# One score for each key place modulo 128 in a windowed attention, ahead of fast-matmul expert layers

## The chip, the cores and the metric

The kernel runs on one core of a Trainium2 chip. The metric is the time of one execution on the device, in microseconds (us).

## What is computed

Three layers follow one another. First an attention over 4 batches of 576 tokens with 8 heads of 64 columns; a query sees its own key and the 127 before it, with a linear distance bias by head:

```python
scores = scale * np.matmul(q, k.transpose(0, 1, 3, 2))
rel = pos[:, None] - pos[None, :]
bias = slopes[:, None, None] * (-np.abs(rel).astype(np.float32))[None, :, :]
mask = (rel >= 0) & (rel < 128)
scores = np.where(mask, scores + bias[None], -1000000000.0)
attn = softmax(scores)
return np.matmul(attn, v)
```

Then a mixture of 8 experts on 2304 tokens of width 512 (`relu(x @ w1[e]) @ w2[e]`, weighed by a gate `P` that comes from `exp(x @ w_gate)` by eight rounds of row and column scaling), and last a two-layer network of hidden width 2048 with a leaky ReLU, whose weights come as float64.

## The kernel before

The tokens are cut into 18 tiles of 128. The attention goes tile by tile, and a tile in two quads of four heads, `steps` being the 36 pairs (tile, quad). A tile's keys are its own block of 128 and the block ahead of it, since the window is 128; where a sequence starts at the tile's first token (tiles 0 and 9) there is one block.

For one quad, `scores` (L594) issues four matmuls of 64 rows into two PSUM tiles `s`, each 2 heads x 256 key places. VectorE adds the slope times the distance, with 2**40 in the masked places, and takes the row's minimum in the same operation (L618); ScalarE takes the exponential and the row sum (L622). `probs_T` (L682) transposes `e` on TensorE, 128 columns at a time, into two PSUM tiles `pt`; ScalarE copies one into `pb` (L693), VectorE the other (L695). `values` (L698) multiplies them with the values into `o` (L708), and at the end of a tile VectorE scales `o` by the spread inverse sums `rb` into `acc` (L716). Tiles in which a sequence starts or which stand just behind a start (four of 18) use a `dist` bias of their own (L571 to L580) and scaled queries.

The expert layers use a seven-product scheme (`PRODUCTS`) for 2 x 2 blocks, in float16 high and low parts. Weights are scaled and split by `Weights` (ScalarE L976, L979, L842; GpSimd L843, L1003), inputs by `Inputs` (L842, L843, L894). `a_steps` (L1128) computes the hidden layer, `b_steps` (L1244) the output, which ScalarE (L1251, L1254), VectorE (L1257) and GpSimd (L1255) add into `acc`. Chunk 0 of expert 0 for the first pairs of tiles is woven into the attention by the list `fill`. `logits(p)` (L736) multiplies a pair's split inputs with the gate weights; for pairs 3 and 4 it is called right after the attention (L1401).

What order all this runs in is set by the class `Plan`: it reads the program's instructions, gives each a cost (`weigh`), finds what depends on what (`depend`), gives each a latest time from the order of TensorE's work (`deadlines`), lists each engine's instructions greedily (`order`), and fixes that list by dependencies. So a change to a cost, or to the program, may move instructions on all engines.

Of the kernel before, what the change touches and what calls it, by code (L numbers as in the profile page):

```python
# [26 lines left out]
FIRST = (0, 1, 3)  # L27
# [3 lines left out]
class Plan:  # L31
# [13 lines left out]
    LANDING = 2000.0  # L45
    PER_NS = 350.0
# [78 lines left out]
    def weigh(self, node, kind, reads, writes):  # L125
# [6 lines left out]
        if "DMA" in kind:  # L132
            sizes = [x[1][0][1] * x[4] * x[3] for x in reads + writes if x[0].split("_")[0] != "in"]
            node["cost"], node["landing"] = max(sizes) / self.PER_NS, self.LANDING
# [30 lines left out]
        elif eng == "Pool":  # L165
            node["cost"] += 190 + 1.89 * n if "float16" in kinds else 185 + 2.12 * n
# [8 lines left out]
    def depend(self, slots, before, after):  # L175
# [11 lines left out]
        for i, node in enumerate(self.nodes):  # L187
# [9 lines left out]
            for name, (r, w) in touched.items():  # L197
# [26 lines left out]
                for mask, k, wrote in seen.get(name, []):  # L224
                    if mask & ((r | w) if wrote else w):
                        found.add(k)
                    if mask & ~w:
                        kept.append((mask & ~w, k, wrote))
# [49 lines left out]
    def order(self, latest):  # L278
# [3 lines left out]
        ready, free = [0.0] * n, dict.fromkeys(self.START, 0.0)  # L282
        waiting = {eng: [] for eng in self.START}
# [23 lines left out]
        def takes(i, t):  # L307
# [3 lines left out]
            if node["eng"] == "PE":  # L311
                cost += self.TURN.get((mode, node["mode"]), 0)
            elif node["shared"] and gpsimd[0] <= t < gpsimd[1]:
                cost = max(cost, gpsimd[1] - t + cost - node["shared"])
            return cost

        for _ in range(n):
# [39 lines left out]
            end = start + cost  # L357
            if eng == "PE":
# [11 lines left out]
            free[eng] = end - (self.START[eng] if cost > 100 else 0)  # L370
            waiting[eng].remove(pick)
# [46 lines left out]
def attn_moe_kernel(  # L418
# [24 lines left out]
    BIG = float(2**40)  # L443
# [43 lines left out]
    qscale = new(const, [P, NP], F32, name="qscale")  # L487
# [13 lines left out]

    for h in range(H):
        r = 64 * (h % 2)
        nc.gpsimd.memset(qscale[r:r + 64, h // 2:h // 2 + 1], -(D ** -0.5) * 2.0 ** (8.0 * (h + 1) / H))


# [25 lines left out]
    def small_psum(shape, name):  # L532
        if "ps_bx" in pools:
# [12 lines left out]
    ramp = new(ap1, [P, 2, 2 * P], F32, tag="e", bufs=4, name="e")  # L546
    dist = ramp[:, 0]
    nc.gpsimd.iota(dist, pattern=[[-1, 2 * P]], base=P, channel_multiplier=1, allow_small_or_imprecise_dtypes=True)
    nc.gpsimd.affine_select(out=dist, in_=dist, pattern=[[1, 2 * P]], base=0, channel_multiplier=-1,
                            compare_op=ALU.is_gt, fill=BIG)  # L550
    nc.gpsimd.affine_select(out=dist, in_=dist, pattern=[[-1, 2 * P]], base=P, channel_multiplier=1,
                            compare_op=ALU.is_ge, fill=BIG)
    slopes = new(ap1, [P, H, 2 * P], F32, name="slopes")
    for h in range(H):
        nc.scalar.activation(out=slopes[:, h], in_=dist, func=AF.Copy, scale=-8.0 * 2.0 ** (-8.0 * (h + 1) / H))

# [5 lines left out]
    def load_qk(i):  # L562
# [5 lines left out]
        st["keys"] = nc.sync.dma_start(k_t[:, :, 0:w], kv[:, :, t0 + P - w:t0 + P])  # L568
        kb = [i] if t0 % S == 0 else [i - 1, i]
        crossed = t0 // S != (t0 + P - 1) // S  # L570
        bias = None  # L571
        if crossed or t0 % S == S - 4 * P:

            bias = new(ap1, [P, 2 * P], F32, tag="dist", name="dist")
            nc.scalar.activation(out=bias, in_=slopes[:, 0], func=AF.Copy, scale=-0.125 * 2.0 ** (8.0 / H))
            if crossed:
                nc.gpsimd.memset(bias[64:128, 0:192], BIG)
            else:
                nc.gpsimd.memset(bias[:, 0:64], BIG)
            nc.gpsimd.tensor_tensor(out=q_t, in0=q_t, in1=qscale.unsqueeze(2).to_broadcast([P, NP, P]), op=ALU.mult)  # L580
        st[i] = dict(k=k_t, qs=q_t, kb=kb, bias=bias)
# [11 lines left out]

    def scores(i, quad):  # L594
        c = st[i]
        kb, qs = c["kb"], c["qs"]
        W = P * len(kb)
        c0 = 2 * P - W
# [5 lines left out]
        e = [new(ap1, [P, 2, 2 * P], F32, tag="e", bufs=4, name="e") for _ in range(2)]  # L604
        c[quad] = dict(e=e)
        for n in range(2):
            for r in range(2):
                h = 4 * quad + 2 * n + r
                ins = nc.tensor.matmul(s[r][:, n, 0:W], qs[64 * r:64 * r + 64, h // 2, :],
                                       c["k"][64 * r:64 * r + 64, h // 2, 0:W], start=True, stop=True)  # L610
        exps = c[quad]["exps"] = []
        for r in range(2):
            for n in range(2):
                h = 4 * quad + 2 * n + r
                bias, scale = slopes[:, h], -0.125
                if c["bias"] is not None:
                    bias, scale = c["bias"], 2.0 ** (-8.0 * (h + 1) / H)
                nc.vector.tensor_tensor_reduce(  # L618
                    out=e[r][:, n, 0:W], in0=s[r][:, n, 0:W], in1=bias[:, c0:], scale=scale,
                    scalar=float(2**41), op0=ALU.add, op1=ALU.min, accum_out=mn[:, 2 * n + r:2 * n + r + 1],  # L620
                )
                ins = nc.scalar.activation(  # L622
                    out=e[r][:, n, 0:W], in_=e[r][:, n, 0:W], func=AF.Exp, bias=mn[:, 2 * n + r:2 * n + r + 1],
                    scale=-1.0, accum_out=sm[:, h:h + 1],
                )
            exps.append(ins)
# [55 lines left out]
    def probs_T(i, quad):  # L682
        c = st[i][quad]
        nb = len(st[i]["kb"])
        c["pb"] = []
        for r in range(2):
            pt = new(ps_t, [P, 2, 2, P], F32, tag="pt", name="pt")
            for n in range(2):
                for b in range(nb):
                    ins = nc.tensor.transpose(pt[:, n, b, :], c["e"][r][:, n, b * P:(b + 1) * P], ident)  # L690
# [842 lines left out]
```

## Time and profile before

| what | value |
|---|---|
| median of three runs | 1840.01 us |
| the three runs | 1840.07, 1840.01, 1834.02 us |
| the profiled execution | 1834.78 us |
| its span, first to last instruction | 1833.0 us |
| TensorE busy | 1807.0 us (99%) |
| ScalarE busy | 1350.1 us (74%) |
| VectorE busy | 1329.2 us (73%) |
| GpSimd busy | 1310.8 us (72%) |
| granted TensorE clock, mean | 0.997 |

PE is TensorE's matmuls, PEld its weight loads, DVE VectorE, ACT ScalarE, POOL GpSimd, SP the engine that issues the loads. The durations of matmuls overlap, so what a matmul costs is read from when the next one starts. The attention lies in the first 177 us of the span.

### The profile page before, as it was taken

Reading aid. Unit: us, or ns where it says so; the run is one execution under the profiler, and the core shown is the slowest. Engines: PE = TensorE matmul, PEld = TensorE weight load, DVE = VectorE, ACT = ScalarE, POOL = GpSimd, SP = SyncE. Lnnn points to the kernel's source line nnn. Section 1 sums busy time; section 2 is a strip of 40 time slices with the busy share of each in tenths; the row PEclk is TensorE's granted clock in tenths of the full one; section 3 lists DMA queues with packets and bytes.
Section 4 is the critical chain, followed back from the end, with each engine's and each line's share of the span. In section 5 each row is a group of like instructions: output and inputs, shape, how many; then the busy total and the mean of one; then the engine's idle time right before and its main releaser. Section 6 shows DMA issues by size and latency. Waiting matters only on the chain.

```text
span 1833.0 us, 45057 instructions
## 1 busy us (share of the span) xinstructions
PE 1807.0 (99%) x17542; PEld 1603.2 (87%) x17542; DVE 1329.2 (73%) x3656; ACT 1350.1 (74%) x3099; POOL 1310.8 (72%) x1154
## 2 busy tenths in 40 slices
PE   8999999999999999999999999999999999999999
PEld 6677888889989898988989898989899888989888
DVE  6877677767777676777777667666666887777877
ACT  8989778767767767767767766667666789877664
POOL 3854778787869777787868777666766796776653
PEclk9999999999999999999999999999999999999999
DMA  8342020202112021202111120100001000101002
GB/s 292 106 130 75 2 82 30 87 19 82 53 47 67 34 73 39 87 19 81 53 47 54 46 82 6 43 24 24 24 24 48 1 25 24 47 2 47 2 33 73
DMA packets 61094, 97.80 MB, mean 53 GB/s; under 512 B 4560, under 2 KB 27600, under 8 KB 60880
## 3 DMA queue, kind: packets, MB, share of 16 engines
q1 hardware_dynamic: 60880, 94.93, 15.7%
q8 instruction: 137, 2.24, 0.5%
q14 instruction: 77, 0.63, 0.1%
HBM read 81.81 MB, written 13.11 MB: 52 GB/s over the span
## 4 chain that ended last, share of the span: by engine, by line
PE 71%; ACT 2%; DVE 2%; DMA 1%; POOL 1%; issue 0%; SPq 0%; ACTq 0%
PE t L1244 36%; PE s L1128 20%; PE sq L1128 15%; DMA raw<-in_moe_w_dram 1%; DVE sx L930 0%; DVE s L1156 0%; ACT acc L917 0%; POOL w L843 0%; ACT junk L976 0%; ACT h L1197 0%; PE xt L916 0%; POOL h L1200 0%; DVE acc L1257 0%; ACT raw L979 0%; ACT q L1140 0%
## 5 line engine op out<-in xcount | busy, mean ns | idle before, releaser
L1244 PE MATMUL t<-w,h 128*128 128x256 f16 x7560 | 949.3, 273 | 5.1 <-ACT acc L1251 3.2
L1128 PEld LDWEIGHTS <-w 128*128 128x128 f16 x8400 | 756.4, 98 | 89.3 <-issue 9.4
L1244 PEld LDWEIGHTS <-h 128*128 128x128 f16 x7560 | 735.1, 98 | 92.6 <-issue 7.5
L1128 PE MATMUL s<-xp,w 128*128 128x256 f16 (+1 forms) x4872 | 591.3, 262 | 2.6 <-ACT q L1140 1.3
L1257 DVE SCALAR_TENSOR_TENSOR acc<-t,pu,acc 128x256 f32<-128x256 f32 x866 | 406.6, 479 | 179.0 <-PE t L1244 151.0
L1200 POOL TENSOR_TENSOR h<-s,h 128x1024 f16<-128x1024 f32 x180 | 383.9, 2133 | 132.1 <-ACT h L1197 76.2
L1128 PE MATMUL sq<-xp,w 128*128 128x256 f16 (+1 forms) x3528 | 429.4, 262 | 1.9 <-DVE s L1156 1.1
L1255 POOL TENSOR_TENSOR acc<-acc,part 128x256 f32<-128x256 f32 x322 | 234.3, 729 | 194.3 <-ACT part L1254 75.7
L843 POOL TENSOR_TENSOR w<-raw,w 128x512 f16<-128x512 f32 x240 | 274.9, 1162 | 46.6 <-ACT w L842 46.4
L1140 ACT ACTIVATE q<-s 128x256 f32<-128x256 f32 x364 | 138.9, 382 | 135.9 <-PE s L1128 133.2
L1197 ACT ACTIVATE h<-s 128x1024 f16<-128x1024 f32 x180 | 190.1, 1056 | 47.0 <-DVE s L1156 45.5
L1156 DVE SCALAR_TENSOR_TENSOR h<-sq,h 128x512 f16<-128x512 f32 x352 | 193.0, 553 | 30.5 <-ACT h L1175 24.4
L1254 ACT ACTIVATE part<-t,pu 128x256 f32<-128x256 f32 x322 | 151.7, 471 | 76.3 <-PE t L1244 71.6
L1144 DVE SCALAR_TENSOR_TENSOR sq<-s,q 128x256 f32<-128x256 f32 x176 | 75.9, 431 | 149.1 <-PE s L1128 91.9
L1144 DVE SCALAR_TENSOR_TENSOR sq<-sq,q 128x256 f32<-128x256 f32 x352 | 150.2, 427 | 37.7 <-PE sq L1128 34.3
L842 ACT ACTIVATE w<-raw 128x512 f16<-128x512 f32 x240 | 148.1, 631 | 12.3 <-PE s L1128 3.9
L1156 DVE SCALAR_TENSOR_TENSOR s<-sq,s 128x256 f32<-128x256 f32 x352 | 146.1, 415 | 0.7
L1175 ACT ACTIVATE h<-sq 128x512 f16<-128x512 f32 x176 | 104.7, 595 | 56.2 <-DVE sq L1144 47.1
L1156 DVE SCALAR_TENSOR_TENSOR s<-sq,q 128x256 f32<-128x256 f32 x352 | 136.7, 417 | 10.6 <-ACT q L1152 8.8
L976 ACT ACTIVATE junk<-raw 128x512 bf16<-128x512 f32 x160 | 100.8, 630 | 11.9 <-DMA raw<-in_moe_w_dram 8.4
L979 ACT ACTIVATE raw<-raw,sr 128x512 f32<-128x512 f32 x160 | 108.4, 719 | 0.1
L1003 POOL TENSOR_TENSOR raw<-raw 128x512 f32<-128x512 f32 x80 | 102.0, 1275 | 0.4 <-DVE dg L819 0.4
(151 smaller groups left out, 1643.1 us busy)
## 6 DMA issues: line engine op xcount, KB each, us to landing
raw<-in_moe_w_dram SPq DMA_DIRECT2D x32, 768.0 KB, 4.7
k_t<-in_k_dram SPq DMA_DIRECT2D x16, 512.0 KB, 4.1
raw<-in_moe_w_dram SPq DMA_DIRECT2D x32, 256.0 KB, 3.6
raw<-in_moe_w_in_dram SPq DMA_DIRECT2D x16, 512.0 KB, 3.6
raw<-in_moe_w_out_dram SPq DMA_DIRECT2D x16, 512.0 KB, 3.5
q_t<-in_q_dram SPq DMA_DIRECT2D x18, 256.0 KB, 3.0
acc<-in_v_dram SPq DMA_DIRECT2D x18, 256.0 KB, 6.0
v_t<-in_v_dram SPq DMA_DIRECT2D x18, 256.0 KB, 2.9
```

The costliest lines, as they stand in the source:

```text
L842: nc.scalar.activation(out=hi, in_=src, func=AF.Copy)
L843: return nc.gpsimd.tensor_tensor(out=lo, in0=src, in1=hi, op=ALU.subtract)
L1128: nc.tensor.matmul(d[b][:, f, :], t[:, wp, kk, ft * P:(ft + 1) * P], XP[p][:, o, kk, xp, :], start=(i == 0 and f == 0 and j in FIRST), sto ...
L1140: nc.scalar.activation(out=q[:, k], in_=ps, func=AF.Copy, scale=CS)
L1144: nc.vector.scalar_tensor_tensor(out=block(k), in0=ps, scalar=CS, in1=q[:, k], op0=ALU.mult, op1=ALU.add)
L1156: nc.vector.scalar_tensor_tensor(out=out, in0=in0, scalar=sc, in1=in1, op0=op0, op1=op)
L1197: nc.scalar.activation(out=h[:, 3:7, 0, :], in_=d["s"], func=AF.Copy)
L1200: nc.gpsimd.tensor_tensor(out=h[:, 3:7, 1, :], in0=d["s"], in1=h[:, 3:7, 0, :], op=ALU.subtract)
L1244: nc.tensor.matmul(ps, h[:, o, hp, f, tt * P:(tt + 1) * P], w[:, wp, ft, :], start=(i == 0 and j in FIRST), stop=(i == 5), skip_group_chec ...
L1254: nc.scalar.activation(out=part, in_=ps, func=AF.Copy, scale=s)
L1255: nc.gpsimd.tensor_tensor(out=dst, in0=dst, in1=part, op=ALU.add)
L1257: nc.vector.scalar_tensor_tensor(out=dst, in0=ps, scalar=s, in1=dst, op0=ALU.mult, op1=ALU.add)
```

## The change

In the attention, a key place of the own block and the same place of the block ahead are never both inside a query's window: own-block keys count up to the query's place, block-ahead keys behind it. The change keeps one score for the two. `scores` still computes 256 places. Then a predicated copy on VectorE writes the scores of the block ahead over those of the own block where the mask `ahead` is 1, in PSUM, for two heads at once. Tiles in which a sequence starts, or behind which one started, get an operation that drops the places outside the sequence. Distance, minimum, exponential, sum and transposes then run on 128 places a head in place of 256. After the transposes, which now fill one PSUM tile for four heads, the probabilities are parted again: ScalarE copies all of them, GpSimd clears the own block's places by an affine selection, and the result goes with the values of the block ahead; VectorE multiplies them by the mask `own` for the values of the own block. The `dist` biases and the scaled queries go.

Besides, the planner gets other constants (DMA landing time and rate, a start time of SP's queue, slower matmuls in its first 11.5 us, a cost of its own for GpSimd's fixed operations) and one rule: two instructions of different engines on one PSUM tile are ordered, reads too. The logits of pairs 3 and 4 move from behind the attention into the list of gating jobs, eight and nine ticks later than they stood; the gate itself starts two ticks earlier.

```diff
-    LANDING = 2000.0
-    PER_NS = 350.0
+    LANDING = 2250.0
+    FIRST = 740.0
+    PAUSE = 1200.0
+    COLD = 11500.0
...
+                    elif mask and name in self.whole and self.nodes[k]["eng"] != node["eng"]:
+                        found.add(k)
...
-    slopes = new(ap1, [P, H, 2 * P], F32, name="slopes")
+    slopes = new(ap1, [P, H, P], F32, name="slopes")
...
-            nc.gpsimd.tensor_tensor(out=q_t, in0=q_t, in1=qscale.unsqueeze(2).to_broadcast([P, NP, P]), op=ALU.mult)
...
+    def drop(x, mask):
+        nc.vector.scalar_tensor_tensor(out=x, in0=spread(mask, x.shape[2]), scalar=-BIG, in1=x, op0=ALU.mult, op1=ALU.add)
...
-        e = [new(ap1, [P, 2, 2 * P], F32, tag="e", bufs=4, name="e") for _ in range(2)]
+        e = [new(ap1, [P, 2, P], F32, tag="e", bufs=6, name="e") for _ in range(2)]
...
         for r in range(2):
+            mine = s[r][:, :, P:2 * P]
+            if at:
+                nc.vector.copy_predicated(mine, spread(ahead, P).bitcast(I32), s[r][:, :, 0:P])
+            if at == 0:
+                drop(mine, ahead)
+            elif S - P < at:
+                drop(mine[64:128], other[64:128])
+            elif at < P:
+                drop(mine[0:64, :, 0:64], ahead[0:64, 0:64])
             for n in range(2):
                 h = 4 * quad + 2 * n + r
...
                 nc.vector.tensor_tensor_reduce(
-                    out=e[r][:, n, 0:W], in0=s[r][:, n, 0:W], in1=bias[:, c0:], scale=scale,
+                    out=e[r][:, n], in0=mine[:, n], in1=slopes[:, h], scale=-0.125,
...
     def probs_T(i, quad):
         c = st[i][quad]
-        nb = len(st[i]["kb"])
-        c["pb"] = []
+        pt = new(ps_t, [P, 4, P], F32, tag="pt", name="pt")
         for r in range(2):
-            pt = new(ps_t, [P, 2, 2, P], F32, tag="pt", name="pt")
             for n in range(2):
-                for b in range(nb):
-                    ins = nc.tensor.transpose(pt[:, n, b, :], c["e"][r][:, n, b * P:(b + 1) * P], ident)
-            pb = new(ap3, [P, 2, 2, P], F32, tag="pb", name="pb")
-            if r == 0:
-                nc.scalar.activation(out=pb[:, :, 0:nb, :], in_=pt[:, :, 0:nb, :], func=AF.Copy)
+                nc.tensor.transpose(pt[:, 2 * r + n, :], c["e"][r][:, n], ident)
+        part = [None, None]
+        for b in range(2 - len(st[i]["kb"]), 2):
+            pb = part[b] = new(ap3, [P, 4, P], F32, tag=f"pb{b}", bufs=2, name="pb")
+            if b == 0:
+                nc.scalar.activation(out=pb, in_=pt, func=AF.Copy)
+                nc.gpsimd.affine_select(out=pb, in_=pb, pattern=[[0, 4], [-1, P]], base=0, channel_multiplier=1,
+                                        compare_op=ALU.is_gt, fill=0.0)
             else:
-                nc.vector.tensor_copy(pb[:, :, 0:nb, :], pt[:, :, 0:nb, :])
-            c["pb"].append(pb)
+                nc.vector.tensor_tensor(out=pb, in0=pt, in1=own.unsqueeze(1).to_broadcast([P, 4, P]), op=ALU.mult)
+        c["pb"] = part[2 - len(st[i]["kb"]):]
...
-    for p in (3, 4):
-        logits(p)
-        tick()
-    gating += [None] * 16 + gate()
+    gating += [None] * 8 + [lambda: logits(3), None, lambda: logits(4)] + [None] * 5 + gate()
```

Counts over the whole program: transposes 272 to 144; reductions of 256 columns 128 to 0, of 128 columns 16 to 144; copies of `pb` on VectorE 36 to 0, products into `pb` 0 to 36; predicated copies 0 to 64; dropping operations 0 to 24; selections of `pb` on GpSimd 0 to 32; query products on GpSimd 4 to 0. The matmuls of the scores, the values, the experts and the network, and the transfers, are the same in number.

The order shows the change at three places. TensorE, early in the attention, before (`s` are scores, `pt` transposes, `o` values, `rt` the spreading of the inverse sums):

```order
L690 MATMUL pt<-ident,e 128x128 x4
L708 MATMUL o<-pb,v_t 64x128 x8
L674 MATMUL rt<-ident,sm 64x128 x8
L609 MATMUL s<-k_t,q_t 128x256 x4
L690 MATMUL pt<-ident,e 128x128 x8
L708 MATMUL o<-pb,v_t 64x128 x8
L690 MATMUL pt<-ident,e 128x128 x4
L609 MATMUL s<-k_t,q_t 128x256 x4
```

and now:

```order
L695 MATMUL pt<-ident,e 128x128 x4
L613 MATMUL s<-k_t,q_t 128x256 x4
L682 MATMUL rt<-ident,sm 64x128 x8
L695 MATMUL pt<-ident,e 128x128 x4
L613 MATMUL s<-k_t,q_t 128x256 x4
L717 MATMUL o<-pb,v_t 64x128 x16
L695 MATMUL pt<-ident,e 128x128 x4
L613 MATMUL s<-k_t,q_t 128x256 x4
```

A quad had eight transposes in two pieces and has four in one; the values follow later, two quads at a time.

VectorE, the scores of one quad, before (an `ISA` row with `e,mn` is the reduction, the one behind it reads its minimum):

```order
L618 ISA e,mn<-s,slopes 128x256
L618 ISA mn 128x1
L618 ISA e,mn<-s,slopes 128x256
L618 ISA mn 128x1
L825 TENSOR_REDUCE k<-mt 128x1
L695 COPY pb<-pt 128x512
```

and now:

```order
L618 COPY_PREDICATED s<-ahead,s 128x2x128 x2
L627 ISA e,mn<-s,slopes 128x128
L627 ISA mn 128x1
L627 ISA e,mn<-s,slopes 128x128
L627 ISA mn 128x1
L627 ISA e,mn<-s,slopes 128x128
L627 ISA mn 128x1
L627 ISA e,mn<-s,slopes 128x128
L627 ISA mn 128x1
L834 TENSOR_REDUCE k<-mt 128x1
L704 TENSOR_TENSOR pb<-pt,own 128x512
```

Two predicated copies stand ahead of four shorter reductions, and the copy of `pb` is a product.

ScalarE, behind the attention's end, before (`xp` are the splits of the last inputs, `acc<-t,pu` evacuates the expert output):

```order
L842 ACTIVATE xp_2803<-acc_111 128x4x128
L842 ACTIVATE xp_2803<-acc_113 128x2x128
L842 ACTIVATE xp_2803<-sx 128x8x128
L842 ACTIVATE xp_2804<-acc_114 128x4x128
L842 ACTIVATE xp_2804<-acc_115 128x2x128
L842 ACTIVATE xp_2804<-h 128x8x128
L1251 ACTIVATE acc_102<-t_2945,pu 128x256
```

and now:

```order
L851 ACTIVATE xp_2729<-acc_110 128x4x128
L851 ACTIVATE xp_2729<-acc_112 128x2x128
L851 ACTIVATE xp_2729<-sx 128x8x128
L851 ACTIVATE xp_2730<-acc_113 128x4x128
L1260 ACTIVATE acc_101<-t_2801,pu 128x256
L851 ACTIVATE xp_2730<-acc_114 128x2x128
L1184 ACTIVATE h<-sq 128x2x256
L1161 ACTIVATE q<-s_2791 128x256
L851 ACTIVATE xp_2730<-h 128x8x128
L1260 ACTIVATE acc_101<-t_2801,pu 128x256
```

The first evacuation stood behind nine splits (three are ahead of these rows) and stands behind seven.

## Rows read from the trace of the kernel before

**Rows 1.** Busy time by stretch: from:to, length, busy us (instructions), clock, DMA, GB/s.
```profile
core 0: us, PE busy (x) PEld busy (x) DVE busy (x) ACT busy (x) POOL busy (x), PEclk, DMA share, GB/s
0.00:37.00 37.00, 29.91 (x255) 22.06 (x255) 24.89 (x114) 29.29 (x103) 7.35 (x24) 0.95 0.94 317
37.00:75.00 38.00, 33.49 (x308) 24.72 (x308) 29.51 (x113) 36.35 (x105) 32.59 (x34) 0.96 0.42 135
75.00:107.00 32.00, 31.60 (x357) 25.62 (x353) 24.56 (x86) 29.02 (x87) 24.91 (x30) 1.00 0.42 135
107.00:137.00 30.00, 29.59 (x284) 22.88 (x281) 22.57 (x82) 27.24 (x89) 10.31 (x15) 1.00 0.32 98
137.00:159.00 22.00, 21.58 (x286) 17.23 (x288) 17.22 (x68) 20.97 (x67) 13.30 (x18) 1.00 0.44 137
159.00:177.00 18.00, 18.00 (x200) 14.34 (x197) 15.16 (x57) 15.58 (x52) 1.00 (x4) 1.00 0.10 27
...
300.00:600.00 300.00, 299.55 (x2906) 269.71 (x2904) 215.92 (x552) 217.31 (x471) 236.31 (x202) 1.00 0.18 57
```

**Rows 2.** Waits of TensorE, 0 to 177 us: total us, times, longest.
```profile
PE s L609 <- DMA k_t<-in_k_dram: 4.6, 1, 4.6
PE pt L690 <- ACT rb L680: 2.5, 2, 1.8
PE pt L690 <- ACT pb L693: 2.1, 2, 1.1
```

**Rows 3.** Timeline, TensorE: start us, length us, line, operation, count.
```profile
170.47 1.09 PE L690 MATMUL pt<-ident,e 128*128 128x128 f32 x8
...
173.17 0.66 PE L690 MATMUL pt<-ident,e 128*128 128x128 f32 x4
```

**Rows 4.** Timeline, VectorE, first quads: reductions one after another.
```profile
5.92 0.29 DVE L618 CUSTOM_DVE_ANT_0 e<-s,slopes 128x128 f32<-128x128 f32 x1 [4.78 <-PE s L609]
6.14 0.29 DVE L618 CUSTOM_DVE_ANT_0 e<-s,slopes 128x128 f32<-128x128 f32 x1
...
11.67 0.42 DVE L618 CUSTOM_DVE_ANT_0 e<-s,slopes 128x256 f32<-128x256 f32 x1
...
12.02 0.42 DVE L618 CUSTOM_DVE_ANT_0 e<-s,slopes 128x256 f32<-128x256 f32 x1
```

**Rows 5.** Timeline, ScalarE, first quads: exponentials one after another.
```profile
6.65 0.39 ACT L622 ACTIVATE e<-e,mn 128x128 f32<-128x128 f32 x1
...
7.04 0.39 ACT L622 ACTIVATE e<-e,mn 128x128 f32<-128x128 f32 x1
...
12.61 0.50 ACT L622 ACTIVATE e<-e,mn 128x256 f32<-128x256 f32 x1
...
13.10 0.49 ACT L622 ACTIVATE e<-e,mn 128x256 f32<-128x256 f32 x1
```

**Rows 6.** Groups by form, whole span: count | busy us, mean ns | idle before.
```profile
L1144 DVE SCALAR_TENSOR_TENSOR sq<-s,q 128x256 f32<-128x256 f32 x176 | 75.9, 431 | 149.1 <-PE s L1128 91.9 <-ACT q L1140 52.7 <-ACT raw L1075 1.3
...
L1172 DVE TENSOR_TENSOR sq<-sq,q 128x512 f32<-128x512 f32 x36 | 25.1, 698 | 5.7 <-ACT q L1171 4.3
...
L695 DVE COPY pb<-pt 128x512 f32<-128x512 f32 x32 | 21.9, 685 | 3.1 <-ACT e L622 1.1 <-PE o L708 1.1 <-PE pt L690 0.3
...
L693 ACT ACTIVATE pb<-pt 128x512 f32<-128x512 f32 x32 | 18.9, 589 | 1.9 <-PE pt L690 1.4
...
L580 POOL TENSOR_TENSOR q_t<-q_t,qscale 128x512 f32<-128x512 f32 x4 | 4.2, 1041 | 30.4 <-DMA k_t<-in_k_dram 17.9 <-PE o L708 7.2 <-PE rt L678 3.4
...
L637 POOL TENSOR_SCALAR_AFFINE_SELECT sel<-sel 128x512 bf16<-128x512 bf16 x3 | 2.0, 667 | 0.2
...
L549 POOL TENSOR_SCALAR_AFFINE_SELECT e<-e 128x256 f32<-128x256 f32 x1 | 0.4, 401 | 0.1
```

**Rows 7.** Timeline behind the attention: TensorE and ScalarE, with idle time before.
```profile
176.37 1.48 PE L1244 MATMUL t<-w,h 128*128 128x256 f16 x12
...
181.78 1.04 ACT L842 ACTIVATE xp<-h 128x1024 f16<-128x1024 f32 x1
...
183.23 2.71 PE L1244 MATMUL t<-w,h 128*128 128x256 f16 x12 [2.94 <-ACT acc L1251]
```

## The prediction before the run

> **What bounds the kernel now.** I read the busy time by stretch first, then the waits, the single instructions, and at last the place behind the attention. From 300 to 600 us TensorE is busy for 299.55 of 300 us [rows 1]: the expert layers run at TensorE's pace, and a change to the attention cannot shorten them. The attention fills the first 177 us. I cut that time where three more of the 18 query tiles have their output; each of the first six rows is such a stage, with three tiles or six quads (a quad is four heads of one tile). In the first two stages TensorE is idle for 37.00 - 29.91 = 7.1 us and 38.00 - 33.49 = 4.5 us; in the other four for 1.2 us in all. The tightest engine beside it is ScalarE: 36.35 of 38.00 us in the second stage, 20.97 of 22.00 in the fifth. Added up over the six stages: ScalarE 158.5 us, VectorE 133.9, GpSimd 89.5, of 177. So VectorE has the most room among the two engines that can read PSUM, and the change moves work onto it. TensorE's longest waits on an engine in this stretch name ScalarE (2.5 us for the spread inverses, 2.1 us for a probability copy, both ahead of transposes) [rows 2].
>
> **TensorE.** 272 transposes become 144: 128 fewer. Eight in a row took 1.09 us and four 0.66 us [rows 3], so one costs (1.09 - 0.66) / 4 = 0.109 us, and 128 cost 14.0 us, 2.3 us a stage. Nothing else on TensorE gets shorter: scores still run over 256 columns and values over both blocks. The Trainium skill, "TensorE: Matmul & The Clock Gate", Part 4, gives about 275 ns for a PE-mode transpose in one kernel; counted that way the saving would be 128 x 0.275 = 35 us (an estimate from that page). By the start times above it is 14.0 us: the page's figure is a latency, and neighbours overlap.
>
> **ScalarE.** 128 of 144 exponentials fall from 256 to 128 columns. They start 0.49 us apart at 256 columns and 0.39 at 128 [rows 5]: 128 x 0.10 = 12.8 us less. The copies of probabilities stay 32 of 512 columns; four 256-wide ones and four bias copies go, some 3 us more at the most. ScalarE: 158.5 - 13 to 16, about 143 us.
>
> **VectorE.** 128 reductions fall from 256 to 128 columns: starts 0.35 us apart against 0.21 [rows 4], so 128 x 0.14 = 17.9 us less. 36 copies become 36 products of 512 columns out of PSUM: 0.698 against 0.685 us [rows 6], 0.5 us more, and 1 us more for the four that were narrow. New are 64 predicated copies of 2 x 128 columns inside PSUM. The trace has none. The nearest row has the same shape, PSUM in and PSUM out: 0.431 us [rows 6], and I take that: 27.6 us. Bounds: below, 0.21 us, the step of the reduction over half the columns, 13.4 us; above, 0.698 us, the product over twice the columns [rows 6], 44.7 us. The Trainium skill, "VectorE: DVE Perf Modes", in its section on the errata, has 120 + FD cycles for a PSUM source, (120 + 256) / 0.96 = 392 ns here, by which the 64 would cost 25.1 us (estimate from that page). 24 masking operations of at most 256 columns, at the same 0.431: 10.3 us. Four one-off masks: 1.7 us at most. Net: -17.9 + 1.5 + 27.6 + 10.3 + 1.7 = +23.2 us, 3.9 us a stage; VectorE goes from 133.9 to 157 us and takes ScalarE's place as the tightest engine beside TensorE.
>
> **GpSimd.** 32 new selections over 512 f32 columns. Such a selection took 0.401 us over 256 columns and 0.667 over 512 of bf16 [rows 6]; so 0.667 to 0.802 for twice 0.401; I take 0.667, the row with as many columns: 21.3 us, 3.6 us a stage (25.7 at the upper end). Four query products of 1.041 us [rows 6] go, two each in stages two and five. That fits into 89.5 of 177 us, but stage two is already at 32.59 of 38.00.
>
> **Chain of a quad.** Before, the two halves of the transposed probabilities lay in two PSUM tiles: ScalarE copied one (0.589 us) while VectorE copied the other (0.685) [rows 6]. Now both read one tile, and the selection follows ScalarE's copy: 0.589 + 0.667 on one side, or 0.589 + 0.698 where the two reads take turns, so about 0.6 us more from transposes to values. Where the expert layers have matmuls to put between, this is covered; that is not so at the very start and in the last stage, whose 18 us hold few of them.
>
> **By stage.** A stage can't be shorter than its fullest engine, which I let run at 95%, the share that ScalarE reached in stages two and five. First: VectorE 24.89 + 3.9 and the 6 us before its first reduction [rows 4] make 35; TensorE 37 - 2.3 = 34.7: -2.0. Second: GpSimd 32.59 + 3.6 - 2.1 = 34.1, VectorE 33.4; over 0.95, 36: -2.0. Third: VectorE 28.5, GpSimd 28.5, so TensorE decides: -2.3. Fourth: VectorE 26.5, TensorE 27.7, -2.3. Fifth: VectorE 17.22 + 3.9 = 21.1, over 0.95 = 22.2: +0.2. Sixth: 15.16 + 3.9 = 19.1, over 0.95 = 20.1: +2.1. Sum -6.3: of TensorE's 14.0 us, 7.7 are not cashed.
>
> **Behind the attention.** TensorE is idle for 2.94 us before 183.23, waiting for ScalarE's first evacuation of the expert output, which stands behind nine splits (the last 1.04 us long); then 12 matmuls take 2.71 us where 12 took 1.48 at 176.37 [rows 7]. With the logits of pairs 3 and 4 later, the order puts that evacuation ahead of the last two splits. It gains at least the last split, 1.0 us, at most 2.94 + 1.23 = 4.2; I take 2.7, between. The 60 small logits matmuls and their three small followers each are the same in number; they fall in a stretch where TensorE has a backlog, and cost nothing unless the gating behind them comes late. The DMAs are the same transfers; the third tile's query and key now go ahead of the first value tile on SP's queue, which I cost at nothing: TensorE waits for a load once, for 4.6 us at the very start [rows 2].
>
> **Sum.** -6.3 - 2.7 = -9.0. The profiled execution took 1834.78 us (span 1833.0), so 1825.8; the three runs have 1834.02, 1840.01 and 1840.07, with the median 5.2 above the profiled one. On the median: 1840.0 - 9.0 = **1831 us**.
>
> **Rivals.**
> *VectorE keeps up.* The planner may spread the expert layers' matmuls so that no stage is VectorE's. Then all 14.0 us count, the waits of [rows 2] go (4.6) and so does the whole end stall (4.2): -22.8, 1817 us. For it: VectorE needs 157 us of some 163. Against it: 96% over the whole stretch, where ScalarE got 89%. Chance 0.19.
> *The chain eats it.* ScalarE's copy and VectorE's product of the one tile take turns, and the selection stands in GpSimd's queue among products of over 1 us: 0.6 us more a quad, exposed in a third of the 36 quads, gives back 7.2 us of the 9.0: 1838 us. For it: no second tile is there any more to read meanwhile. Against: TensorE was idle for 1.2 us only in the last four stages, so it has other matmuls to put there. Chance 0.24. The Trainium skill, "PSUM — Partial Sum Buffer", in the section on PSUM bank collisions, says that two engines must not access the same partitions of one bank at the same time, whether or not they touch the same bytes; by that the turns are forced. No row of before shows two engines at one tile of probabilities.
> *Slower: predicated copies near their upper bound.* At 0.698 us VectorE needs another 64 x 0.267 = 17.1 us, 174 in all; at 95% with the 6 us of the start that is 189 us where the attention had 177: +12 - 2.7, 1849 us. It turns where the attention's gain is gone: VectorE at 163 us, 0.53 us a copy. For it: no row of before holds that operation. Against: the PSUM rows follow their columns (0.431 at 256, 0.698 at 512). Chance 0.12.
> That the change does less than it says can be excluded for the counts, which the order shows.
>
> **Numbers.** Forecast 0.45 (1820 to 1836), keeping up 0.19, chain 0.24, slower 0.12. Changes under about 0.5% (9.2 us) can't be told from none here. Faster by more, under 1830.8: 0.19 and 0.6 of 0.45, together 0.46 (its lower side is longer, since the range of the end stall and of the copies reach further down). Same: the other 0.18, and the chain's 0.24, less 0.02: 0.40. Slower: 0.14. The range 1814 to 1843 leaves out the slower case and a little at the lower end.
>
> **What would show it.** Right: transposes 144 and the attention's last output at 170 to 173 us; VectorE over 88% busy in the last two stages, ScalarE under 85%; TensorE's waits there naming VectorE; the 2.94 us wait gone or halved. Wrong: VectorE under 80% with TensorE waiting on GpSimd's selection (the chain), a predicated copy over 0.53 us (slower), or the attention ending before 165 us with TensorE at 97% (keeping up). The end of the program, from 300 us on, should be as before within 2 us; if it is not, the new order outside the attention is the cause, which I have not priced.

## The result, and the profile after

The changed kernel takes 1815.87 us (median of four runs, 1815.47 to 1816.65) where the kernel before took 1837.31 beside it (four runs, 1834.02 to 1840.07). The ratio is 0.9885, 95% interval 0.9867 to 0.9904; a second comparison (whole_again, below) gave 0.9894 (0.9881 to 0.9907). It is faster by 1.1%, 21 us by the medians, where 9 were forecast. By the profiled executions it is 18.7 us: 1834.78 to 1816.09, spans 1833.0 and 1814.4.

Busy time by stretch, after, cut again where three more tiles have their output, with a stretch of the expert layers at the end (compare [rows 1]):

```profile
core 0: us, PE busy (x) PEld busy (x) DVE busy (x) ACT busy (x) POOL busy (x), PEclk, DMA share, GB/s
0.00:33.20 33.20, 26.26 (x225) 20.11 (x227) 24.11 (x121) 23.30 (x94) 7.67 (x18) 1.00 0.90 292
33.20:74.10 40.90, 37.61 (x314) 27.02 (x310) 35.03 (x159) 36.54 (x121) 32.12 (x36) 0.83 0.58 188
74.10:107.70 33.60, 32.40 (x340) 26.31 (x337) 29.81 (x114) 30.48 (x100) 29.44 (x35) 0.95 0.45 143
107.70:132.80 25.10, 24.24 (x242) 19.03 (x240) 21.29 (x86) 21.48 (x72) 12.14 (x17) 1.00 0.30 97
132.80:155.50 22.70, 22.33 (x282) 17.25 (x283) 21.25 (x97) 21.34 (x84) 19.00 (x26) 1.00 0.36 109
155.50:169.00 13.50, 13.45 (x164) 11.02 (x163) 11.66 (x39) 7.37 (x25) 3.32 (x8) 1.00 0.10 35
286.00:586.00 300.00, 299.37 (x2904) 269.39 (x2902) 215.44 (x548) 217.64 (x471) 237.10 (x202) 1.00 0.18 57
```

The attention ends at 169.0 us, with the last scaling of `o` into `acc`, where it ended at 177.3. Summed over it, VectorE is busy for 143.2 us, ScalarE for 140.5, GpSimd for 103.7; before, 134.2, 158.5 and 89.5. So VectorE took 9 us more, not the 23.2 of the forecast. The stretch of the expert layers is as full as before. TensorE's idle time up to the attention's end is the same, 12.8 us before ([rows 1]) and 12.7 after; its busy time fell from 164.2 to 156.3 us, by 8 us where 14.0 us of transposes went. The granted clock was 0.83 in the second stage and 0.95 in the third, where no stage before was under 0.95; the last section comes back to that.

TensorE's waits from 0 to 169 us, after (total us, times, longest):

```profile
PE s L613 <- DVE mn L627: 5.8, 6, 1.6
PE s L613 <- DMA k_t<-in_k_dram: 5.0, 1, 5.0
PE mt L832 <- DVE dg L828: 0.7, 1, 0.7
PE pt L695 <- ACT e L631: 0.7, 1, 0.7
```

The two waits that named ScalarE [rows 2] are gone. In their place TensorE waits for VectorE's reductions, which hold the PSUM tile that the next scores need: 5.8 us. No wait names GpSimd's selection.

Groups of the new and the shortened operations, after, whole span (count | busy us, mean ns | idle before):

```profile
L627 DVE CUSTOM_DVE_ANT_0 e<-s,slopes 128x128 f32<-128x128 f32 x144 | 34.0, 285 | 0.9 <-PE pt L695 0.6
L618 DVE COPY_PREDICATED s<-ahead,s 128x256 f32<-128x256 int32 x64 | 24.8, 425 | 10.7 <-PE s L613 10.3
L704 DVE TENSOR_TENSOR pb<-pt,own 128x512 f32<-128x512 f32 x36 | 24.3, 683 | 1.3 <-ACT pb L700 1.0 <-ACT rb L688 0.2
L597 DVE SCALAR_TENSOR_TENSOR s<-other,s 64x256 f32<-64x256 f32 x8 | 3.2, 438 | 0.1
L701 POOL TENSOR_SCALAR_AFFINE_SELECT pb<-pb 128x512 f32<-128x512 f32 x32 | 20.6, 648 | 38.4 <-ACT pb L700 37.6 <-DVE s L1165 0.5
L631 ACT ACTIVATE e<-e,mn 128x128 f32<-128x128 f32 x144 | 56.0, 392 | 11.6 <-DVE mn L627 9.4 <-PE rt L682 2.0
```

A predicated copy takes 0.425 us, next to the 0.431 that was taken for it; a selection 0.648, next to 0.667; a product 0.683, next to 0.698 [rows 6]. The prices were right for one instruction alone. Neighbours overlap, though, as the timeline of VectorE, after, shows (start us, length us):

```profile
34.34 0.42 DVE L618 COPY_PREDICATED s<-ahead,s 128x256 f32<-128x256 int32 x1
34.67 0.15 DVE L843 TENSOR_SCALAR sr<-k 128x1 int32<-128x1 int32 x1
34.73 0.42 DVE L618 COPY_PREDICATED s<-ahead,s 128x256 f32<-128x256 int32 x1
```

The instruction behind the copy starts 0.33 us after it, not 0.42. If each moment is counted once, for the instruction that was there first, the 64 copies take 23.8 us of VectorE's time (0.371 each).

Behind the attention, after: TensorE, then ScalarE, with the idle time before (compare [rows 7]):

```profile
171.37 0.82 PE L1137 MATMUL sq<-xp,w 128*128 128x256 f16 x6
173.65 0.82 PE L1253 MATMUL t<-w,h 128*128 128x256 f16 x6 [1.46 <-ACT acc L1260]
175.79 0.81 PE L1253 MATMUL t<-w,h 128*128 128x256 f16 x6 [1.33 <-DVE acc L1266]
...
172.62 0.61 ACT L851 ACTIVATE xp<-acc 128x512 f16<-128x512 f32 x1
173.14 0.45 ACT L1260 ACTIVATE acc<-t,pu 128x256 f32<-128x256 f32 x1
```

The wait of 2.94 us has become 1.46, and a second one of 1.33 for VectorE stands behind it.

A difference that no step of the forecast holds lies near the end of the program, where the last network begins. Waits of TensorE from 1430 to 1560 us, before:

```profile
PE xt L916 <- DVE k L828: 1.6, 1, 1.6
PE t L1244 <- DVE acc L1257: 1.3, 2, 0.9
PE sq L1128 <- DVE s L1156: 0.7, 2, 0.4
```

Busy time there, before, and then after (its stretch with nearly the same matmuls begins 14 us earlier):

```profile
1430.00:1560.00 130.00, 125.83 (x1182) 112.05 (x1181) 107.24 (x309) 111.97 (x245) 103.46 (x81) 1.00 0.05 18
```

```profile
1416.00:1540.00 124.00, 123.98 (x1180) 111.85 (x1177) 106.30 (x309) 109.98 (x245) 103.21 (x81) 1.00 0.05 19
```

1180 matmuls take 124 us where 1182 took 130, and the 4.2 us in which TensorE was idle there are gone. So some 5 of the 18.7 us of the profiled executions, over a quarter, lie 1250 us behind the attention.

### The profile page after: what moved, and what is told of

Same layout as the page of the kernel before. It is cut to its first block, busy times and chain, and to the rows that moved or that the text cites. A ratio compares the mean times of both kernels' runs of the same rounds, so it can differ in the third digit from the quotient of the medians.

```text
span 1814.4 us, 45033 instructions
## 1 busy us (share of the span) xinstructions
PE 1794.3 (99%) x17414; PEld 1595.6 (88%) x17414; DVE 1341.7 (74%) x3748; ACT 1330.1 (73%) x3091; POOL 1325.5 (73%) x1170
## 4 chain that ended last, share of the span: by engine, by line
PE 91%; DMA 3%; DVE 2%; ACT 2%; POOL 1%; issue 1%; SPq 0%; POOLq 0%; ACTq 0%; DVEq 0%
PE t L1253 42%; PE s L1137 25%; PE sq L1137 18%; PE s L613 2%; PE o L717 2%; DMA raw<-in_moe_w_dram 1%; DMA raw<-in_moe_w_in_dram 1%; PE pt L695 1%; PE xt L925 0%; PE rt L682 0%; POOL raw L1090 0%; ACT junk L985 0%; DVE s L1165 0%; POOL w L852 0%; POOL raw L1086 0%
```

## Experiments: the parts alone

The change was taken apart: the attention, the planner's rule for two engines on one PSUM tile, the planner's constants and costs, and the place of the logits. The planner makes a new order for each kernel. The kernels were compared in three groups, each beside the kernel before, so rows are compared by their ratios; by the intervals, two rows have to differ by some 3 to 5 us to be told apart. The last column is (1 - ratio) x 1836 us, about the median of before in the three groups.

| kernel | attention | rule | constants | logits | ratio to before (95%) | us gained |
|---|---|---|---|---|---|---|
| rule_only | old | new | old | old | 0.9976 (0.9965 to 0.9988) | 4.4 |
| consts_only | old | old | new | old | 0.9972 (0.9961 to 0.9984) | 5.1 |
| plan_only | old | new | new | old | 0.9940 (0.9922 to 0.9958) | 11.0 |
| logits_only | old | old | old | new | 0.9968 (0.9956 to 0.9979) | 5.9 |
| plan_logits | old | new | new | new | 0.9952 (0.9938 to 0.9966) | 8.8 |
| attn_rule | new | new | old | old | 0.9969 (0.9955 to 0.9983) | 5.7 |
| no_logits | new | new | new | old | 0.9922 (0.9903 to 0.9940) | 14.3 |
| whole_again | new | new | new | new | 0.9894 (0.9881 to 0.9907) | 19.5 |

**attn_rule**, the attention with the rule:

```diff
-    LANDING = 2250.0
-    FIRST = 740.0
-    PAUSE = 1200.0
-    COLD = 11500.0
+    LANDING = 2000.0
+    FIRST = 0.0
+    PAUSE = 0.0
+    COLD = 0.0
...
-    gating += [None] * 8 + [lambda: logits(3), None, lambda: logits(4)] + [None] * 5 + gate()
+    for p in (3, 4):
+        logits(p)
+        tick()
+    gating += [None] * 16 + gate()
```

The costs of transfers and of GpSimd's fixed operations are back as well.

> The new attention with the planner's old constants and the logits back behind the attention; of the planner's edits only the rule for two engines on one PSUM tile stays. Theory 1 (the attention pays by itself, 12 us ahead of 300 us, of which 3 to 4 hang on the logits; the 6 us of TensorE's idle time near 1440 to 1550 us are the planner's): 8 to 10 us faster than before, ratio 0.9945 to 0.9955, and the idle time near 1440 to 1550 us still 5 to 7 us. Theory 2 (the gain is the planner's new order, the transposes were hidden): within 4 us of before, ratio 0.998 to 1.002. Theory 3 (the late idle time goes with the attention, by whatever reordering it brings): 15 to 18 us faster, ratio 0.990 to 0.992.

It gained 5.7 us, between theories 1 and 2, and TensorE was busy for all of 1430 to 1560 us, so the idle time there is gone without the constants. Since rule_only gains 4.4 without the new attention, the attention adds 1.3 here, less than the intervals can tell from nothing. Theory 1 falls in this form.

**plan_only**, the old attention with the planner of the change:

```diff
+                    elif mask and name in self.whole and self.nodes[k]["eng"] != node["eng"]:
+                        found.add(k)
...
+        free["SP"] = self.FIRST
...
-                cost += self.TURN.get((mode, node["mode"]), 0)
+                cost += self.TURN.get((mode, node["mode"]), 0) + (0.9 * cost if t < self.COLD else 0)
```

These are three places of its edit, which is the whole class `Plan` of the change, with all constants and costs.

> The old attention and the old place of the logits, with all of the planner's edits. Theory 1: the 6 us of idle time near 1440 to 1550 us go and little else changes: 5 to 7 us faster than before, ratio 0.996 to 0.9973. Theory 2 (the gain is the planner's): 14 us faster or more, ratio under 0.9925. Theory 3 (the planner's edits do nothing): within 2 us, ratio 0.999 to 1.001.

11.0 us: more than theory 1 had, short of theory 2, and by itself half of the whole gain, from a part that the forecast put at nothing.

**rule_only** and **consts_only**, which split it:

```diff
+                    elif mask and name in self.whole and self.nodes[k]["eng"] != node["eng"]:
+                        found.add(k)
```

(and, for consts_only, the new class without these two lines)

> The kernel before with one edit: the planner's rule that orders two engines on one PSUM tile, reads too. Theory 1 (the rule's order removes TensorE's 6 us of idle time near 1440 to 1550 us, the constants act in the first 200 us): 5 to 7 us faster, ratio 0.996 to 0.9975, that idle time under 1 us, the first 200 us as before. Theory 2 (the constants do both): within 2 us of before, ratio 0.999 to 1.001, that idle time still 5 to 7 us.

> The kernel before with the planner's constants and costs of the change, without the rule. Theory 1: 3 to 6 us faster, ratio 0.9967 to 0.9985, by TensorE's idle time in the first 60 us, and the idle time near 1440 to 1550 us still 5 to 7 us. Theory 2: as all of the planner's edits together, 10 to 11 us faster, ratio 0.9935 to 0.9945, that idle time gone.

The same two stretches of time, rule_only first, then consts_only:

```profile
0.00:60.00 60.00, 48.77 (x434) 35.68 (x435) 44.40 (x196) 51.98 (x169) 25.89 (x44) 0.97 0.74 247
1430.00:1560.00 130.00, 129.43 (x1225) 116.32 (x1224) 110.92 (x320) 115.01 (x256) 108.49 (x86) 1.00 0.05 18
```

```profile
0.00:60.00 60.00, 51.39 (x475) 38.27 (x475) 47.43 (x208) 54.03 (x175) 30.67 (x48) 1.00 0.79 260
1430.00:1560.00 130.00, 125.77 (x1181) 111.90 (x1179) 106.56 (x301) 112.76 (x248) 105.90 (x83) 1.00 0.05 18
```

With the rule, TensorE is idle for 0.6 us of the late stretch and gets 1225 matmuls done; without it, 4.2 us and 1181, as before. With the constants, the first 60 us hold 475 matmuls where before held 430 in 49.85 us of busy time, and TensorE's waits for ScalarE there (2.5 and 2.1 us, [rows 2]) are gone; 3.5 us for VectorE's reductions stand there now, and the granted clock is 1.00 where it was 0.95. So the rule works in the late stretch and the constants in the first 60 us. The traces do not show how the rule's order removes the late waits for VectorE; that stays open.

**logits_only** (the lines of the change's last hunk alone), **no_logits** (the change without them) and **plan_logits** (the change without its attention):

```diff
-    for p in (3, 4):
-        logits(p)
-        tick()
-    gating += [None] * 16 + gate()
+    gating += [None] * 8 + [lambda: logits(3), None, lambda: logits(4)] + [None] * 5 + gate()
```

> The old attention and planner, with the logits of pairs 3 and 4 in the list of gating jobs. Theory 1: the wait of 2.94 us for ScalarE's first evacuation behind the attention goes or is halved, 2 to 4 us faster, ratio 0.998 to 0.999. Rival: the wait goes on to the next evacuation, within 1 us, ratio 0.9995 to 1.0005.

> The whole change but for the logits, which are back behind the attention. Theory 1: the wait behind the attention is there again, 2 to 4 us slower than the whole change, ratio to before 0.9905 to 0.9915 where the whole change has 0.9885. Rival: it is not, ratio 0.988 to 0.9895.

> The whole change but for the attention, which is the old one. The planner alone gave 10.7 us, the logits alone 5.7, the attention (with the rule) alone 5.0, by the medians; they add up to the 21.4 of the whole change. Theory A (the parts add up): 16 us faster than before, ratio 0.991, and so 5 us slower than the whole change. Theory B (the attention's 14 us of transposes come through once the other parts are there): 7 to 8 us faster, ratio 0.996. Theory C (the attention is worth nothing beside the others): as the whole change, ratio 0.9885.

On the kernel before, the logits gain 5.9 us; the wait of 2.94 us is 0.8 there. On top of the planner they gain nothing (0.9940 and 0.9952, intervals overlapping). On top of planner and attention they gain 5.2 to 6.8 us (0.9922 to 0.9894 and 0.9885; the intervals overlap by a little). The attention, in turn, gains 1.3 us on the rule and 3.3 on the planner, neither clear of nothing, and 10.7 to 12.3 on planner and logits, which is. The parts do not add up (theory A falls); theory B is nearest, its 7 to 8 us against 8.8 for plan_logits.

The profiles show two places where the parts meet. The first is inside the attention, over which the busy times of plan_only and plan_logits are:

```profile
0.00:171.30 171.30, 161.72 (x1679) 126.18 (x1680) 133.31 (x516) 157.46 (x498) 89.39 (x121) 1.00 0.49 161
```

```profile
0.00:177.50 177.50, 164.10 (x1685) 127.54 (x1686) 137.38 (x517) 157.79 (x498) 89.31 (x121) 0.98 0.48 155
```

The old attention ends at 171.3 us with the new planner alone, 6 us earlier than before, and at 177.5 with the logits moved as well: there TensorE is idle for 13.4 us in place of 9.6, at a clock of 0.98 in place of 1.00. The wait behind the attention is shorter in plan_logits too (1.5 us in place of 2.9), but the order has lost more ahead of it. The new attention ends at 169.0 us, so most of the 10.7 to 12.3 us that it gains is gained over this 177.5. Why the order of plan_logits is the longer one is not shown.

The second place is behind the attention's end. In no_logits the attention ends at 168.8 us, as in the whole change, but with 1524 matmuls done where the whole change has done 1557. From 168 to 180 us, no_logits, and then the whole change:

```profile
168.00:180.00 12.00, 5.93 (x37) 4.09 (x37) 11.51 (x16) 6.15 (x11) 10.12 (x7) 0.86 0.00 1
```

```profile
168.00:180.00 12.00, 9.21 (x113) 8.04 (x111) 10.48 (x24) 10.12 (x22) 10.23 (x9) 1.00 0.01 2
```

37 matmuls where 113 were done. Timeline of no_logits there, TensorE, VectorE and GpSimd, and in the last line VectorE in the whole change:

```profile
176.34 0.26 PE L832 MATMUL mt<-dg,ones 128*128 128x128 bf16 x1 [4.49 <-DVE dg L828]
...
172.89 2.34 DVE L903 TENSOR_TENSOR h<-acc,h 128x256 f32<-128x256 f32 x1
175.15 1.14 DVE L828 TENSOR_SCALAR dg<-identb,e 128x128 bf16<-128x128 bf16 x1
...
176.85 2.15 DVE L828 TENSOR_SCALAR dg<-identb,e 128x128 bf16<-128x128 bf16 x1
...
172.65 2.30 POOL L852 TENSOR_TENSOR xp<-sx,xp 128x1024 f16<-128x1024 f32 x1
...
176.84 2.12 POOL L852 TENSOR_TENSOR xp<-sx,xp 128x1024 f16<-128x1024 f32 x1
...
168.89 0.24 DVE L828 TENSOR_SCALAR dg<-identb,e 128x128 bf16<-128x128 bf16 x1
```

TensorE waits 4.49 us for a `dg`, a link of the chain that scales the next inputs. In no_logits this `dg` stands in VectorE's queue behind six other instructions that follow the attention's last output, and starts 7 us after that output began (168.04 us); in the whole change it stands right behind the output. So here the planner's order gives part of the attention's gain back. (The profiled execution of no_logits, 1826.74 us, is 4 above its median, so the wait may be shorter in others.)

## Experiments: the load of each engine

**twice_turned** gives TensorE its transposes back:

```diff
                 nc.tensor.transpose(pt[:, 2 * r + n, :], c["e"][r][:, n], ident)
+                if len(st[i]["kb"]) == 2:
+                    nc.tensor.transpose(pt[:, 2 * r + n, :], c["e"][r][:, n], ident)
```

> The whole change with 128 transposes more: each of the tiles with a block ahead is transposed twice into the same place, so that TensorE has the 272 of before again and the other engines the work of after. Theory A (each transpose counts, since TensorE always has other matmuls to do): 13 to 15 us slower than the whole change, ratio to before 0.996 to 0.997. Theory B (as the forecast had it, half is hidden, since VectorE is the tightest engine): 5 to 8 us slower, ratio 0.991 to 0.993. Theory C (all hidden behind VectorE): within 2 us, ratio 0.988 to 0.990.

Ratio 0.9958 (0.9944 to 0.9972), 11.8 us slower than whole_again, so 84% of the 14.0 us: near theory A. Busy time over its attention:

```profile
0.00:178.50 178.50, 161.76 (x1673) 128.66 (x1674) 148.84 (x608) 141.84 (x490) 104.45 (x137) 0.98 0.49 155
```

The 11.8 us are not the price of the transposes alone. Compared with whole_again (its line stands below), the attention is 9.4 us longer, TensorE's busy time only 5.3, at a clock of 0.98 in place of 0.95, and its idle time 4.1; VectorE's busy time rose by 5.7 us with no work added.

**copy_half** and **copy_twice** load VectorE:

```diff
                 nc.vector.copy_predicated(mine, spread(ahead, P).bitcast(I32), s[r][:, :, 0:P])
+                if r == 0:
+                    nc.vector.copy_predicated(mine, spread(ahead, P).bitcast(I32), s[r][:, :, 0:P])
```

(copy_twice: without the condition)

> The whole change with every second predicated copy done twice (32 more, the second writes the same scores), so that VectorE has some 12 us more in the attention, 155 us, about the load that the forecast had put there. Theory A (VectorE's load costs nothing below its capacity, since TensorE has other matmuls): within 2 us of the whole change. Theory B (the forecast's step by stage: a stage can't be shorter than its fullest engine at 95%): 6 to 9 us slower than the whole change.

> The whole change with all 64 predicated copies done twice, VectorE with some 25 us more in the attention, 168 us where the attention has 169. Theory A: VectorE is now past what the stretch holds in several stages, 4 to 8 us slower than the whole change. Theory B: 17 to 22 us slower, nearly the whole of the added work.

> The whole change once more, unedited, beside the others of this chip. Its ratio to before was 0.9885 in the first comparison; both theories expect 0.987 to 0.990 again, and the three kernels beside it are compared with this one.

copy_half: 0.9949 (0.9938 to 0.9961), 10.1 us slower than whole_again. copy_twice: 0.9981 (0.9973 to 0.9990), 16.0 us slower. Busy time over the whole attention, whole_again, copy_half and copy_twice:

```profile
0.00:169.10 169.10, 156.49 (x1557) 120.77 (x1558) 143.15 (x608) 140.51 (x490) 103.65 (x137) 0.95 0.51 163
```

```profile
0.00:178.40 178.40, 155.62 (x1554) 119.33 (x1555) 157.36 (x639) 141.93 (x490) 103.33 (x137) 0.93 0.49 155
```

```profile
0.00:185.40 185.40, 161.60 (x1551) 123.67 (x1552) 165.72 (x667) 141.82 (x490) 102.45 (x137) 0.93 0.46 149
```

VectorE is busy for 14.2 and 22.6 us more, and the cost is 10.1 and 16.0 us. Counted as above, each moment once, the added copies are 10.4 and 20.7 of it; the rest is other instructions that ran longer. So the first half of the copies is paid for nearly in full, both together to three quarters, each give or take 3 us. Theory A falls: this load is not covered, though VectorE was busy for only 85% of the attention. Theory B is nearer, too low for copy_half (6 to 9) and too high for copy_twice (17 to 22). In copy_half TensorE's longest waits name it (7.1 us in four waits for the reductions). A second copy lengthens a quad's chain as well as VectorE's load, and the clock is lower too (0.93 for 0.95); these runs do not part the three.

**bias_tables** moves 20 of the 24 drops to GpSimd:

```diff
+            bias = new(ap1, [P, H, P], F32, tag="bias", name="bias")
+            nc.gpsimd.affine_select(out=bias, in_=slopes, ..., compare_op=ALU.is_ge, fill=BIG)
...
-                    out=e[r][:, n], in0=mine[:, n], in1=slopes[:, h], scale=-0.125,
+                    out=e[r][:, n], in0=mine[:, n], in1=c["bias"][:, h], scale=-0.125,
```

> The whole change with 20 of the 24 dropping operations on VectorE replaced by bias tables that GpSimd makes for five tiles (all but the first of those at a sequence's start), so VectorE has some 6 to 7 us less and GpSimd some 8 us more. Theory A (VectorE's load is covered): within 2 us of the whole change. Theory B (VectorE sets the stages): 3 to 6 us faster.

In this kernel the masked places of these five tiles differ from the reference's. Ratio 0.9947 (0.9929 to 0.9964), 9.8 us slower than whole_again; neither theory. VectorE's busy time fell by 2.5 us in place of 6 to 7 (140.6 over the attention), and GpSimd's rose by 10.5 (114.1). So it is no clean test of a smaller VectorE load. TensorE now waits for GpSimd's selection (1.4 us in three waits), which no wait named in the whole change, so GpSimd's time may not be free here; what makes up the 9.8 us is not shown. No run beats the whole change.

## Why the prediction was right, and where it was not

The sign and the range held (1815.9 in 1814 to 1843), the time did not: 1831 was forecast, from a kernel before of 1840.0 that took 1837.3 here, and the gain was over twice its 9.0 us. That the range held is luck in part: it reached down to 1814 for other reasons than those that brought the time there. By its steps:

- **TensorE, 14.0 us.** Right as a price: four transposes take 0.60 to 0.66 us, as in [rows 3] (whose (1.09 - 0.66) / 4 is 0.108, so 13.8 us), and putting them back costs 11.8 us. The 275 ns of the Trainium skill, "TensorE: Matmul & The Clock Gate", Part 4, 35 us in all, would have been far too much. What the step left out is the clock: TensorE's busy time in the attention fell by only 8 us, where more of it was at the lower level (the estimate is in the last section).
- **ScalarE.** Forecast 13 to 16 us less, measured 17.9 (158.5 to 140.5). **GpSimd.** Forecast 21.3 more for the selections and 4.2 less for the query products, so 17.1; the selections took 20.6, and the sum is 14.2 more.
- **VectorE, +23.2 us to 157.** This term failed: +9.0, to 143.2. Counting each moment once, the reductions fell by 20.2 (forecast 17.9), the copies cost 23.8 (27.6), the drops 7.8 (10.3), the products 0.2 (1.5), the one-off masks 0.8 (1.7), and other work in the stretch fell by 3.4. What was added had been priced by the length of an instruction, and what was removed by the step from start to start, which is shorter where neighbours overlap. That explains some 4 of the 14.2 us (64 copies of 0.425 us are 27.2, and took 23.8); the rest is spread over drops that were shorter than assumed, reductions that saved more, and other work.
- **By stage, 7.7 of 14.0 us not cashed.** Its input was wrong, and its rule looks too mild. With VectorE at the forecast's 157 us, copy_half is where plan_logits is, with the old attention (0.9949 and 0.9952): if the load is what costs there, and not the longer chain, all of the gain would have been lost, not 7.7 us. With the real 143, the attention gains 10.7 to 12.3 us beside the other parts. The two errors lie in opposite directions. In the profiled executions the attention ends 8.3 us earlier with all edits together, where 6.3 were forecast for this step, and the 5.7 us not cashed have another form than the step gave them: TensorE is idle as long as before and at the lower clock for longer. Signs: the attention's end came at 169.0, short of 170 to 173; VectorE was 94% and 86% busy in the last two stages (over 88% was said), ScalarE 94% and 55% (under 85% was said), and the one wait of TensorE there, 1.2 us, names VectorE.
- **Behind the attention, 2.7 us.** The mechanism was right, and the wait halved; a fixed price was wrong. The logits gave nothing to 6.8 us, by what else was in the kernel.
- **The planner, not priced.** The largest miss. The text said that from 300 us on nothing would change by over 2 us, and that otherwise the order outside the attention is the cause. That holds for the late stretch, which is rid of its idle time in rule_only too. And plan_only gains 11.0 us, of which some 6 are in the attention (it ends at 171.3 us). What the forecast did price, attention and logits, gains 8.5 to 10.1 us on top of plan_only (0.9940 to 0.9894 and 0.9885), so its 9.0 was about right, by errors that cancelled.
- **The rivals.** *VectorE keeps up* named the time, 1817, but not for its reasons: a wait of 5.8 us for VectorE is there, the stall at the end is not gone (1.46 and 1.33 us), and plan_only alone has half of the gain. *The chain eats it*: in the whole change no wait of TensorE names the selection; it falls. VectorE's product did wait for ScalarE's copy of the same tile, but for 1.0 us in all. The Trainium skill, "PSUM — Partial Sum Buffer", in the section on PSUM bank collisions, by which the two must take turns, is not tested by this, since the new rule sets their order anyway. *Predicated copies*: 0.425 us, far from 0.53.

Open are how the rule's order removes the late waits, why plan_logits loses in the attention what plan_only gains there, and whether the price of VectorE's load is its queue, the chain or the clock.

## What to carry to other kernels

Where a planner sets the order, an edit of its rules is an edit of the whole program: price it, or run it alone first, and look for idle time of the bounding engine far from the code that was changed. Take the cost of added instructions, like that of removed ones, from start to start. Do not add up the gains of parts: here the same attention was worth 1 to 12 us by what else stood in the kernel, since each edit gets a new order of the whole program. And when an engine's work shrinks, look at its clock as well as at its idle time.

## What was not expected of the hardware

TensorE's clock fell in the second stage of the attention and stayed low while it waited. Windows of time, after, then its timeline there, with 16 small matmuls at the upper level (the line of 34.54 us) against 14 of the same kind at the lower (51.60):

```profile
36.00:40.00 4.00, 3.19 (x35) 2.27 (x31) 3.68 (x16) 4.00 (x11) 3.50 (x6) 1.00 1.01 367
40.00:42.00 2.00, 1.89 (x8) 1.24 (x9) 1.97 (x11) 2.00 (x8) 2.00 (x3) 0.62 1.09 355
42.00:44.00 2.00, 1.48 (x8) 0.76 (x4) 1.71 (x4) 2.00 (x9) 2.00 (x3) 0.50 0.92 295
...
52.00:54.00 2.00, 2.00 (x19) 1.54 (x16) 1.99 (x12) 0.38 (x2) 1.49 (x3) 0.50 0.00 0
54.00:56.00 2.00, 2.00 (x26) 1.54 (x24) 0.15 (x1) 1.67 (x8) 2.00 (x3) 0.97 0.00 0
...
34.54 1.09 PE L682 MATMUL rt<-ident,sm 128*64 128x128 f32 x16
...
39.71 1.63 PE L695 MATMUL pt<-ident,e 128*128 128x128 f32 x4 [0.66 <-ACT e L631]
...
45.12 2.46 PE L613 MATMUL s<-k_t,q_t 64*128 64x256 f32 x8 [1.64 <-DVE mn L627]
...
51.60 1.76 PE L682 MATMUL rt<-ident,sm 128*64 128x128 f32 x14
```

From 42 to 54 us the granted clock was 0.50, the level of 1.2 GHz. Before it fell, TensorE was busy for 3.19 of 4.00 us, with a wait of 0.66 us for ScalarE; while it was low, TensorE waited another 1.64 us for VectorE. An estimate from the mean clocks: 0.83 over 40.9 us and 0.95 over 33.6 us are some 17 us at the lower level, where [rows 1] has some 7 (0.95 over 37 us, 0.96 over 38). By the two lines above, work takes up to twice as long there, so the 10 us more cost at most 5 us, about what is missing between the 14.0 us of transposes and the 8 us by which TensorE's busy time fell. whole_again has the same 0.83 in that stage.

VectorE's `dg`, 0.25 us in most of its 51 places in the whole change (1.24 at the most), took 1.14 and 2.15 us in no_logits. The longer one began within 0.01 us of a GpSimd operation of 2.12 us and ended 0.04 us after it, as the rows above show, and TensorE waited for the shorter one. The Trainium skill, "GPSIMD Engine Reference", section 1, has the two engines share their SBUF interfaces, with contention where VectorE runs a two-port mode or reads two SBUF inputs. The rows agree with a contention; they do not show which of the two cases it was.
